# Second-half down product in fp16 terms with on-chip powers of two

## The chip, the cores and the metric

One core of one Trainium2 chip runs the whole program. The metric is the device time of one execution in microseconds (us). Three executions of the kernel before gave 1748.77, 1750.04 and 1750.48 us, median 1750.04. The result is float32 and is compared with the reference in float32, so the kernel carries each large product as two or three terms of fewer bits.

## The reference

2048 tokens of width 576 go through two branches, and a gate per token mixes them:

```python
g = sigmoid((x * gate_w).sum(-1, keepdims=True))
a = _A_ref(x, A_wq, A_wk, A_wv, A_wo, A_beta)      # attention in 4 segments, 32 heads of 18, with a memory
b = (silu(x @ w_gate) * (x @ w_up)) @ w_down       # 576 -> 4608 -> 576
return g * a + (1 - g) * b
```

The change is in the last product, `(silu * up) @ w_down`, for one half of the tokens.

## The kernel before

A first stage (up to about 233 us in the profiled execution) projects Q, K and V. Then the 4608 features are taken as 36 tiles of 128, and the tokens as two halves of 1024: the first half runs f = 0 to 35, then the second half does so. What follows calls them first and second half. A last stage multiplies the attention output by `wo`, mixes and stores.

For each feature tile f the loop does seven products (a Strassen scheme over gate and up, each 7 matmuls of 512 columns, in three fp16-term products plus a rest). Between them stand eight calls of `tick()`. A tick first issues what was put off to it (`defer(k, fn)` puts a function k ticks ahead), then some groups of the down product, then a step of the attention. So all engines' instructions stand in one program order which the ticks set; an engine works its own instructions strictly in that order. f mod 3 is called q below.

The row of the seven products and what reads them, with the lines of the profile: ScalarE copies the first sum (L1381), the second (L1384), the fourth (L1391) and the fifth (L1395); VectorE adds at L1388 and L1396; after the fifth product come the two Silu activations (L1398 and L1400). Silu and Exp stand in different activation tables, so in the second half each f then loads the Exp table back (`exp_table()`, L1297) for the attention. After the seventh product VectorE multiplies (L1406, L1407).

The down product of three feature tiles (a chunk, `CH = 3`) is done as 16 groups in the ticks of the next f with q = 0: 8 token tiles by two column parts of 320 and 256. Each group is 9 matmuls (3 tiles by 3 terms) into one of two banks, and VectorE adds the bank to the sum `ya` (L1098). The operands are pairs of fp32r terms: `hh`, `hl` from the product (ScalarE rounds at L1188 or L124, VectorE subtracts at L1189 or L125), and the two terms of `w_down`, made in the first half (L1070, L1071), stored to DRAM as `dc`, and fetched back in the second half by `d_fetch`. SyncE issues these transfers.

The attention runs in steps that a credit per tick paces: 0.76 of a step per tick without down groups, 1 with them. A step writes score tiles (L957 transposed scores, L846 scores) into banks 5, 6 and 7 in rotation (`ts_tile`); a bank is free again once ScalarE has taken the exponential (L961) or VectorE the maximum (L864, L854). GpSimd does the differences of the terms (L1058, L903).

`power(out, t)` (L140 to L146) turns a sum of squares into a power of two: one matmul with ones adds over the partitions, and four VectorE instructions on 128x1 make the power. The kernel before uses it for x and for the gate and up weights; `iw` holds the inverse scales.

## Time and profile before

| | us |
|---|---|
| median of 3 runs | 1750.04 |
| profiled execution, its own time | 1750.37 |
| its span, first to last instruction | 1748.7 |
| second half, from its first product to the end of f = 34 | 933 to 1646 |
| attention steps end, about | 1580 |

In the views, "idle before" is the time in which an engine stood still before an instruction, and the name after the arrow is what it waited for. Matmuls are pipelined: what one costs is the distance from one start to the next, not its printed duration. Weight loads (PEld) run beside matmuls. The profiler's clock row shows the TensorE clock as granted: 0.998 of full speed over the span.

### The profile page before, as it was taken

How to read it: one execution, taken by the hardware profiler on the slowest of the kernel's cores; microseconds unless marked ns; L12 is line 12 of the kernel's file. 1: busy time of each engine (PE TensorE's matmuls, PEld its weight loads, DVE VectorE, ACT ScalarE, POOL GpSimd, SP SyncE). 2: the span in 40 equal slices, each digit the busy share in tenths (PEclk: the TensorE clock that was granted, in tenths of full speed). 3: DMA queues.
4: the chain of work that ended last, by engine and by line, in shares of the span. 5: the costliest groups of instructions: out<-in, count | busy, mean ns of one | idle time of the engine just before them, and what ended most of it. 6: DMA issues, size and time to landing. Idle time of an engine off the chain costs nothing.

```text
span 1748.7 us, 34878 instructions
## 1 busy us (share of the span) xinstructions
PE 1714.6 (98%) x12241; PEld 1217.6 (70%) x12241; DVE 1326.4 (76%) x3239; ACT 1024.4 (59%) x1800; POOL 841.7 (48%) x1065
## 2 busy tenths in 40 slices
PE   9999999999999999999999999999999999999999
PEld 7889856666766676567656757766756766776699
DVE  6677676788878888888886877778778777775455
ACT  6756575767676666655754565566456466455411
POOL 3325552255545554665542764555546565553121
PEclk9999999999999999999999999999999999999999
DMA  8656776776687666545554477587577569654544
GB/s 284 224 211 225 237 244 206 224 234 191 179 247 225 205 186 193 185 142 153 169 165 150 123 181 182 132 207 170 125 185 196 143 147 210 167 125 129 184 137 139
DMA packets 341667, 321.89 MB, mean 184 GB/s; under 512 B 193396, under 2 KB 258676, under 8 KB 341492
## 3 DMA queue, kind: packets, MB, share of 16 engines
q1 hardware_dynamic: 341492, 319.67, 63.1%
q8 instruction: 96, 1.57, 0.4%
q14 instruction: 79, 0.65, 0.1%
HBM read 188.51 MB, written 104.86 MB: 168 GB/s over the span
## 4 chain that ended last, share of the span: by engine, by line
PE 79%; DVE 7%; ACT 5%; DMA 3%; issue 3%; SPq 2%; POOL 1%; DVEq 0%; ACTq 0%; POOLq 0%
PE bank L1304 33%; PE bank L1089 23%; PE bank L172 7%; PE bank L1307 5%; PE bank L846 4%; PE bank L957 2%; PE bank L985 2%; PE bank L987 1%; DMA stw<-q 1%; PE bank L919 1%; ACT L1297 1%; DVE xo L1242 1%; PE bank L460 1%; ACT L1398 1%; DMA wo__21835<-wc 0%
## 5 line engine op out<-in xcount | busy, mean ns | idle before, releaser
L1089 PE MATMUL bank<-dw,hh 128*128 128x320 f32 (+1 forms) x2304 | 510.0, 314 | 9.2 <-DVE ya L1098 7.0
L1089 PEld LDWEIGHTS bank<-dw,hh 128*128 128x128 f32 x2304 | 380.3, 190 | 35.0 <-DVE ya L1098 11.1
L1089 PE MATMUL bank<-dw,hl 128*128 128x320 f32 (+1 forms) x1152 | 341.0, 296 | 0.6 <-DVE hl L125 0.5
L1058 POOL TENSOR_TENSOR p<-pe,p 128x512 f16<-128x512 f32 x220 | 273.5, 1243 | 88.1 <-DVE p L1056 60.6
L961 ACT ACTIVATE pe<-bank 128x512 f32<-128x512 f32 x220 | 130.8, 594 | 222.3 <-PE bank L957 197.6
L1098 DVE TENSOR_TENSOR ya<-bank,ya 128x320 f32<-128x320 f32 x352 | 157.5, 453 | 90.1 <-PE bank L1089 87.2
L1089 PEld LDWEIGHTS bank<-dw,hl 128*128 128x128 f32 x1152 | 218.4, 190 | 1.1 <-DVE hl L125 1.1
L1307 PE MATMUL bank<-xr,rh 128*128 128x512 f16 x504 | 191.0, 379 | 0.0
L969 POOL TENSOR_SCALAR_AFFINE_SELECT pe<-pe 128x256 f32<-128x256 f32 (+1 forms) x220 | 92.4, 420 | 188.5 <-ACT pe L961 184.6
L864 DVE CUSTOM_DVE_ANT_0 junk<-bank,cm 128x128 bf16<-128x128 f32 (+2 forms) x352 | 169.8, 483 | 15.0 <-PE bank L846 10.0
L318 POOL TENSOR_TENSOR ws<-raw 128x256 f32<-128x256 f32 x72 | 67.5, 938 | 153.2 <-DMA raw<-in_wf_dram 91.3
L846 PE MATMUL bank<-kst,qst 108*128 108x512 bf16 (+3 forms) x512 | 125.2, 300 | 5.4 <-ACT pe L961 2.1
L1189 DVE TENSOR_TENSOR hl<-row,hh 128x512 fp32r<-128x512 f32 x120 | 110.9, 924 | 16.3 <-ACT hh L1188 16.1
L1056 DVE CAST p<-pe 128x512 f16<-128x512 f32 x220 | 108.2, 492 | 0.1
L1391 ACT ACTIVATE row<-bank 128x512 f32<-128x512 f32 x72 | 43.1, 598 | 106.8 <-PE bank L1307 106.6
L957 PE MATMUL bank<-qst,kst 111*128 111x512 bf16 (+3 forms) x352 | 104.2, 303 | 0.0
L1396 DVE TENSOR_TENSOR row<-bank,row 128x512 f32<-128x512 f32 x72 | 49.7, 691 | 70.7 <-ACT bank L1395 70.3
L172 PE MATMUL bank<-xo,qhi 128*128 128x512 f32 x288 | 91.9, 399 | 0.6 <-DVE xo L125 0.5
L1307 PEld LDWEIGHTS <-rh 128*128 128x128 f16 x504 | 49.3, 98 | 59.5
L1395 ACT ACTIVATE bank<-bank 128x512 f32<-128x512 f32 x72 | 41.9, 582 | 83.1 <-PE bank L1307 81.2
L416 POOL TENSOR_TENSOR q<-qr,q 128x512 bf16<-128x512 f32 x36 | 47.1, 1308 | 82.7 <-ACT q L415 70.2
L903 POOL TENSOR_TENSOR xo<-xr,xo 128x512 f16<-128x512 f32 x60 | 71.0, 1184 | 21.7 <-DVE xo L902 12.4
(1067 smaller groups left out, 4121.8 us busy)
## 6 DMA issues: line engine op xcount, KB each, us to landing
xo<-in_wf_dram SPq DMA_DIRECT2D x65, 320.0 KB
dc<-dw SPq DMA_DIRECT2D x36, 576.0 KB
dw<-dc SPq DMA_DIRECT2D x36, 576.0 KB
raw<-in_wf_dram SPq DMA_DIRECT2D x72, 256.0 KB
rh<-rc SPq DMA_DIRECT2D x72, 168.0 KB
draw<-in_wd_dram SPq DMA_DIRECT2D x36, 288.0 KB
xo<-in_xT_dram SPq DMA_DIRECT2D x33, 256.0 KB
vd<-vps SPq DMA_DIRECT2D x8, 912.0 KB
```

Source lines behind the costliest of these rows:

```text
L172: nc.tensor.matmul(t, st[n], mv[n], start=(n == 0), stop=(n == 13))
L846: nc.tensor.matmul(t[:, c:c + w], qs[:KR, pr, P * i:P * i + P], ks[:KR, pr, 0:w], start=True, stop=True)
L864: nc.vector.tensor_tensor_reduce(junk.bitcast(BF)[:, :w], t[:, c:c + w], cm[:, L - w:L], 1.0, -3.0e38, OP.add, OP.max, m[:, k:k + 1])
L957: nc.tensor.matmul(t[:, c:c + w], ks[:KR + 3, pr, P * j:P * j + P], qs[:KR + 3, pr, P * j:L], start=True, stop=True)
L961: nc.scalar.activation(pe, t, AF.Exp, scale=SCALE)
L1056: nc.vector.tensor_copy(p1, pe)
L1058: nc.gpsimd.tensor_sub(p2, pe, p1)
L1089: nc.tensor.matmul(t, p, q[:, cs], start=(f == CH * c and n == 0), stop=(f == CH * c + CH - 1 and n == 2))
L1098: nc.vector.tensor_add(ya[:, i, cs], t, ya[:, i, cs])
L1189: defer(k + 1, lambda: nc.vector.tensor_sub(lo, src, f32(hi)))
L1304: nc.tensor.matmul(t, w[:, p, z], x[z][:, q], start=first and n == 0, stop=False, skip_group_check=True)
L1307: nc.tensor.matmul(t, rem[:, RPOS[j]], XR[j], start=False, stop=True, skip_group_check=True)
```

## The change

In the second half the down product takes fp16 terms instead of fp32r ones. For this:

- `w_down` is no longer stored as terms in the first half. The second half loads the raw tiles, squares and sums them (`look`, ScalarE), finds a power of two for each chunk with `power`, and makes the fp16 terms `high` (ScalarE) and `low` (VectorE) in the free half of the same tile.
- The product `silu * up` is left in fp32 by the multiplies; each tile is squared and summed (`h_look`), and at q = 2 a second power of two per chunk is found and the terms of its tiles are made, 1024 columns at a time (`h_plan`).
- The eviction multiplies by the inverse of both powers, as one instruction with the add.
- The chunks of the second half are shifted: [0, 1], [2, 3, 4], ... [32, 33, 34], [35], so there are 13 instead of 12, and the last two are done in the last stage.

The first half keeps its fp32r product.

```diff
-    dc = dram.tile([FT, P, 2 * D], F32, name="dc")
...
-            defer(3, lambda: nc.sync.dma_start(dc[f], f32(d).rearrange("p a n -> p (a n)")))
...
+            if half:
+                inv = norms[fs[0]][2]
+                if fs[0] == 0:
+                    nc.vector.tensor_scalar_mul(ya[:, i, cs], t, inv)
+                else:
+                    nc.vector.scalar_tensor_tensor(ya[:, i, cs], t, inv, ya[:, i, cs], op0=OP.mult, op1=OP.add)
+                return
...
+        def d_plan(fs):
...
+            def load(f):
+                nc.sync.dma_start(at[f][0], wd[f])
+            def look(f):
+                nc.scalar.activation(dd[CH].bitcast(F16)[:, :D], at[f][0], AF.Square, accum_out=column(f % CH))
+            def high(f):
+                nc.scalar.activation(at[f][1][:, 0], at[f][0], AF.Copy, scale=sd)
+            def low(f):
+                nc.vector.scalar_tensor_tensor(at[f][1][:, 1], at[f][0], sd, at[f][1][:, 0], op0=OP.mult, op1=OP.subtract)
+            a, b = min(f % CH for f in fs), max(f % CH for f in fs) + 1
+            return load, look, lambda: total(sd, a, b), lambda: power(sd, ts_tile([P, 1])), high, low
+        def h_look(f, b, src):
+            nc.scalar.activation(junk, src, AF.Square, scale=iw[f // 4], accum_out=column(3 + 2 * (f % CH) + b))
+        def h_plan(fs):
...
+            def scales():
+                power(sh, ts_tile([P, 1]))
+                for i in at:
+                    nc.vector.tensor_mul(by[i], sh, iw[i])
+            def inverse():
+                nc.vector.tensor_mul(inv, sh, sd)
+                nc.vector.reciprocal(inv, inv)
+            def high(f):
+                t = terms(fp.tile([P, 2, L], F32R, name="hh" if f == FT - 1 else "hl"))
+                raw = hs[1, f]
...
+                nc.scalar.activation(hs[1, f][0], raw, AF.Copy, scale=by[f // 4])
+            def low(f):
+                hi, lo, raw = hs[1, f]
+                hs[1, f] = hi, lo
+                nc.vector.scalar_tensor_tensor(lo, raw, by[f // 4], hi, op0=OP.mult, op1=OP.subtract)
...
+        CHUNKS = [[f for f in range(c, c + CH) if 0 <= f < FT] for c in range(-1, FT, CH)]
...
+            if half and q == 0:
+                fs = CHUNKS[f // CH]
+                load, look, dt, dp, high, low = d_plan(fs)
+                plan += [((0, 1, 4)[n], lambda g=g, fn=load: fn(g)) for n, g in enumerate(fs)]
+                plan += [(5 + n, lambda g=g, fn=look: fn(g)) for n, g in enumerate(fs)]
+                plan += [(9, dt), (10, dp)]
+                for n, g in enumerate(fs):
+                    plan += [(11 + n, lambda g=g, fn=high: fn(g)), (12 + n, lambda g=g, fn=low: fn(g))]
...
+            if half and q == 2:
+                fs = CHUNKS[f // CH]
+                ht, hp, hi, high, low = h_plan(fs)
+                plan += [(2, ht), (3, hp), (4, hi)]
+                for n, g in enumerate(fs):
+                    plan += [(4 + n, lambda g=g, fn=high: fn(g)), (5 + n, lambda g=g, fn=low: fn(g))]
...
-                elif (q, k) in ((1, 0), (1, 2), (2, 1)):
-                    g = f - 1 if k == 0 else f
-                    ds[half, g] = d_fetch(g)
...
-            nc.vector.tensor_mul(sg0, xx, sg0)
-            nc.vector.tensor_mul(sg1, p5, sg1)
-            if q == CH - 1:
+            nc.vector.tensor_mul(hh[:, 0] if half else sg0, xx, sg0)
+            nc.vector.tensor_mul(hh[:, 1] if half else sg1, p5, sg1)
+            if half:
+                for b in range(2):
+                    defer(2 + b, lambda b=b, f=f, t=hh: h_look(f, b, t[:, b]))
+            elif q == CH - 1:
...
-            split_by(3, hh[:, 1], hl[:, 1], sg1)
+            if half == 0:
+                split_by(3, hh[:, 1], hl[:, 1], sg1)
```

Three places of the order. First, ScalarE at the boundary from f = 26 (q = 2) to f = 27 (q = 0) of the second half, before: `bank` is a product's sum, `pe` the attention's exponential, `row` a Silu, `bg` the dummy that goes with the Exp table.

```order
L1395 ACTIVATE bank_19691<-bank_19520 128x512
L961 ACTIVATE pe<-bank_19700 128x512
L1398 ACT_TABLE_LOAD
L1398 ACTIVATE row<-row,sc 128x512
L1400 ACTIVATE row<-bank_19611,sc 128x512
L1297 ACT_TABLE_LOAD
L1297 ACTIVATE bg<-idt 128x1
L961 ACTIVATE pe<-bank_19732 128x512
L1381 ACTIVATE bank_19758<-bank_19756 128x512
L124 ACTIVATE hh<-row 128x512
L961 ACTIVATE pe<-bank_19775 128x512
```

The same place of the change (L1486 was L1395, L960 was L961, L1489 and L1491 the Silus, L1368 was L1297, L1472 was L1381):

```order
L1486 ACTIVATE bank_19805<-bank_19629 128x512
L1172 ACTIVATE hl<-hh,sc 128x1024
L960 ACTIVATE pe<-bank_19818 128x512
L1489 ACT_TABLE_LOAD
L1489 ACTIVATE row<-row,sc 128x512
L1491 ACTIVATE row<-bank_19717,sc 128x512
L1368 ACT_TABLE_LOAD
L1368 ACTIVATE bg<-idt 128x1
L1172 ACTIVATE hl<-hh,sc 128x1024 x2
L960 ACTIVATE pe<-bank_19857 128x512
L1472 ACTIVATE bank_19882<-bank_19880 128x512
L1151 ACTIVATE junk,sc<-hh,sc 128x512
```

One `high` of the product's terms (L1172) now stands ahead of the Silu, and two stand behind the second table load, ahead of the exponential that came first there.

Second, VectorE at the same boundary in the change (L1177 is `low`, L1497 and L1498 were L1406 and L1407, L863 was L864). Before, the maxima L864 came straight after L1407.

```order
L1177 SCALAR_TENSOR_TENSOR hl<-hh,sc,hl 128x1024 x2
L1497 TENSOR_TENSOR hh<-bank_19805,row 128x512
L1498 TENSOR_TENSOR hh<-row 128x512
L1177 SCALAR_TENSOR_TENSOR hl<-hh,sc,hl 128x1024
L863 ISA junk,mb_2435<-bank_19859,cm 128x256
```

Two `low` now stand ahead of the closing multiplies and one behind them, ahead of the maxima.

Third, ScalarE at the boundary from f = 10 (q = 1) to f = 11 (q = 2) in the change; L1142 is `high` of `w_down`, L1151 is `h_look`, and the row that stood before between L1381 and the exponential was L1188 (`hh<-row`).

```order
L1486 ACTIVATE bank_14987<-bank_14810 128x512
L1142 ACTIVATE dw<-dw,sc 128x576
L960 ACTIVATE pe<-bank_14998 128x512
L1489 ACT_TABLE_LOAD
L1489 ACTIVATE row<-row,sc 128x512
L1491 ACTIVATE row<-bank_14852,sc 128x512
L1368 ACT_TABLE_LOAD
L1368 ACTIVATE bg<-idt 128x1
L1142 ACTIVATE dw<-dw,sc 128x576
L1472 ACTIVATE bank_15035<-bank_15033 128x512
L1151 ACTIVATE junk,sc<-hh,sc 128x512
L960 ACTIVATE pe<-bank_15051 128x512
```

Of the chunk's three `high` the first stands a few rows ahead of this piece, the second behind L1486 and the third behind the second table load. The `low` of the third stands on VectorE ahead of L1497.

More of the change, by code (lines that the diff above doesn't have):

```diff
@@ L1071, in d_split @@
             defer(2, lambda: nc.vector.scalar_tensor_tensor(d[:, 1], r, k, f32(d[:, 0]), op0=OP.mult, op1=OP.subtract))
-            defer(3, lambda: nc.sync.dma_start(dc[f], f32(d).rearrange("p a n -> p (a n)")))
-            return d
-        def d_fetch(f):
-            d = d_tile()
-            nc.sync.dma_start(f32(d).rearrange("p a n -> p (a n)"), dc[f])
             return d
         def down_part(t, g, a, b):
-            c, i, hf, hs, ws, half = g
+            fs, i, hf, half = g
             bl, k = divmod(i, 4)
             cs = (slice(0, 320), slice(320, D))[hf]
-            for f in range(CH * c + a, CH * c + b):
+            for f in fs[a:b]:
                 hh, hl = (z[:, bl, P * k:P * k + P] for z in hs[half, f])
-                d = ws[half, f]
+                d = ds[half, f]
                 dh, dl = d[:, 0], d[:, 1]
                 for n, (p, q) in enumerate(((hh, dh), (hh, dl), (hl, dh))):
-                    nc.tensor.matmul(t, p, q[:, cs], start=(f == CH * c and n == 0), stop=(f == CH * c + CH - 1 and n == 2))
+                    nc.tensor.matmul(t, p, q[:, cs], start=(f == fs[0] and n == 0), stop=(f == fs[-1] and n == 2))
         def down_end(t, g):
-            c, i, hf, hs, ws, half = g
+            fs, i, hf, half = g
             ya = yas[half]
             cs = (slice(0, 320), slice(320, D))[hf]
-            if c == 0:
+            if half:
[5 more added lines that the diff above has]
+                return
+            if fs[0] == 0:
                 nc.vector.tensor_copy(ya[:, i, cs], t)
@@ L1098, in down_end @@
                 nc.vector.tensor_add(ya[:, i, cs], t, ya[:, i, cs])
-            if c == FT // CH - 1 and hf and half == 0:
+            if fs[-1] == FT - 1 and hf:
                 stores.append((ffd[i], ya[:, i]))
@@ L1105, in down_groups, with column, terms @@
             for t, g in todo:
-                down_part(t, g, 0, CH - 1 if n > 1 else CH)
+                down_part(t, g, 0, len(g[0]) - (n > 1))
             for t, g in todo:
                 if n > 1:
-                    down_part(t, g, CH - 1, CH)
+                    down_part(t, g, len(g[0]) - 1, len(g[0]))
                 down_end(t, g)
+        norms = {}
+        dd = []
+        def column(k):
+            return sc[:, k:k + 1]
+        def terms(t):
+            return f32(t).rearrange("p a n -> p (a n)").bitcast(F16)
@@ new lines, in d_place @@
+        def d_place(f):
+            if f == FT - 1:
+                return fp.tile([P, D], F32, name="draw", bufs=2), dd[CH].bitcast(F16).rearrange("p (z n) -> p z n", z=2)
+            t = f32(dd[f % CH])
+            return t[:, 0], t[:, 1].bitcast(F16).rearrange("p (z n) -> p z n", z=2)
+        def d_plan(fs):
+            k = CHUNKS.index(fs) % 2
+            norms[fs[0]] = [column(20 + 8 * k + j) for j in range(5)]
+            sd = norms[fs[0]][0]
+            at = {f: d_place(f) for f in fs}
+            for f in fs:
+                ds[1, f] = at[f][1]
+            def load(f):
[8 more added lines that the diff above has]
+            return load, look, lambda: total(sd, a, b), lambda: power(sd, ts_tile([P, 1])), high, low
@@ new lines, in h_look @@
+        def h_look(f, b, src):
+            nc.scalar.activation(junk, src, AF.Square, scale=iw[f // 4], accum_out=column(3 + 2 * (f % CH) + b))
+        def h_plan(fs):
+            sd, sh, inv, *ks = norms[fs[0]]
+            at = sorted({f // 4 for f in fs})
+            by = {i: ks[n] for n, i in enumerate(at)}
+            a, b = 3 + 2 * min(f % CH for f in fs), 5 + 2 * max(f % CH for f in fs)
+            def scales():
[8 more added lines that the diff above has]
+                raw = hs[1, f]
+                hs[1, f] = [t[:, 2 * L * z:2 * L * z + 2 * L].rearrange("p (a n) -> p a n", a=2) for z in range(2)] + [raw]
+                nc.scalar.activation(hs[1, f][0], raw, AF.Copy, scale=by[f // 4])
[3 more added lines that the diff above has]
+                nc.vector.scalar_tensor_tensor(lo, raw, by[f // 4], hi, op0=OP.mult, op1=OP.subtract)
+            return lambda: total(sh, a, b), scales, inverse, high, low
@@ L1210, in beat, with feed @@
                         c_open()
-        def feed(half, f):
-            return [(f // CH, i, hf, hs, ds, half) for i in range(8) for hf in range(2)]
+        CHUNKS = [[f for f in range(c, c + CH) if 0 <= f < FT] for c in range(-1, FT, CH)]
+        def feed(half, fs):
+            return [(fs, i, hf, half) for i in range(8) for hf in range(2)]
         def x_second(new, z):
@@ L1317, in gated_mix @@
             if q == 0 and f:
-                groups += feed(half, f - 1)
+                groups += feed(half, CHUNKS[f // CH - 1] if half else list(range(f - CH, f)))
             plan = []
+            if half and f == 0:
+                dd += [d_tile() for _ in range(CH)] + [fp.tile([P, D], F32, name="draw", bufs=2)]
+            if half and q == 0:
[6 more added lines that the diff above has]
+                    plan += [(11 + n, lambda g=g, fn=high: fn(g)), (12 + n, lambda g=g, fn=low: fn(g))]
+            if half and f == FT - 2:
+                load, look, dt, dp, high, low = d_plan(CHUNKS[-1])
+                plan += [(o, lambda fn=fn: fn(FT - 1)) for o, fn in ((1, load), (5, look), (9, high), (10, low))]
+                plan += [(7, dt), (8, dp)]
+            if half and q == 2:
[4 more added lines that the diff above has]
+                    plan += [(4 + n, lambda g=g, fn=high: fn(g)), (5 + n, lambda g=g, fn=low: fn(g))]
             if nxt:
@@ L1375, in gated_mix @@
             hh = fp.tile([P, 2, L], F32R, name="hh")
-            hl = fp.tile([P, 2, L], F32R, name="hl")
-            hs[half, f] = hh, hl
+            if half:
+                hs[half, f] = hh = f32(hh)
+            else:
+                hl = fp.tile([P, 2, L], F32R, name="hl")
+                hs[half, f] = hh, hl
             a, y, xx = a_tile(), y_tile(), x_tile()
@@ L1405, in gated_mix @@
             seven(xx, 6, False)
-            nc.vector.tensor_mul(sg0, xx, sg0)
-            nc.vector.tensor_mul(sg1, p5, sg1)
-            if q == CH - 1:
+            nc.vector.tensor_mul(hh[:, 0] if half else sg0, xx, sg0)
+            nc.vector.tensor_mul(hh[:, 1] if half else sg1, p5, sg1)
+            if half:
+                for b in range(2):
+                    defer(2 + b, lambda b=b, f=f, t=hh: h_look(f, b, t[:, b]))
+            elif q == CH - 1:
                 defer(2, lambda t=(hh[:, 0], hl[:, 0], sg0): split(*t))
@@ L1417, in gated_mix @@
             if f == FT - 1:
-                groups += feed(half, f)
                 if half == 0:
+                    groups += feed(half, list(range(FT - CH, FT)))
                     for n in range(BREAK):
@@ L1425, in gated_mix @@
                     assert not groups
+        groups += feed(1, CHUNKS[-2]) + feed(1, CHUNKS[-1])
         while due:
@@ L1437, in gated_mix @@
         ops = None
+        total_, scales, inverse, high, low = h_plan(CHUNKS[-1])
+        last = {1: (total_, scales, inverse), 2: (lambda: high(FT - 1), lambda: low(FT - 1))}
         def downs(k):
@@ L1454, in gated_mix @@
                 nxt = c_tr(*tiles.pop(n))
+                for fn in last.get(n, ()):
+                    fn()
                 downs(2 if n else 4)
```

## The prediction

> **What bounds the kernel now.** I read the page first: how busy each engine is, and on which engine the chain that ended last lies.

> ```profile
> PE 1714.6 (98%) x12241; PEld 1217.6 (70%) x12241; DVE 1326.4 (76%) x3239; ACT 1024.4 (59%) x1800; POOL 841.7 (48%) x1065
> PE 79%; DVE 7%; ACT 5%; DMA 3%; issue 3%; SPq 2%; POOL 1%; DVEq 0%; ACTq 0%; POOLq 0%
> ```

> TensorE (PE) is busy all the time. Since a busy PE may still be waiting inside modelled ends, I read next what PE waited for in the second half alone (933 to 1646 us), the view of waits:

> ```profile
> PE bank L846 <- DMA kst<-stw: 2.0, 1, 2.0
> PE bank L1089 <- DVE ya L1098: 1.0, 3, 0.4
> PE bank L1304 <- DMA wo__21823<-wc: 0.7, 1, 0.7
> PE bank L846 <- ACT pe L961: 0.7, 2, 0.4
> ```

> These are the largest of seven, and all make some 5 us out of 713. So each microsecond taken from PE's own stream counts in full, and so does each new wait. Third, the windows of one chunk, f = 24, 25 and 26 (columns: PE, PEld, DVE, ACT, POOL busy, clock, DMA share):

> ```profile
> 1417.80:1454.10 36.30, 36.30 (x307) 28.91 (x305) 27.51 (x89) 16.30 (x28) 18.39 (x27) 1.00 0.55 117
> 1454.10:1465.70 11.60, 11.60 (x59) 5.51 (x58) 8.30 (x22) 8.62 (x15) 8.27 (x12) 1.00 1.04 295
> 1465.70:1480.20 14.50, 14.50 (x144) 7.98 (x143) 11.14 (x30) 10.45 (x18) 7.43 (x10) 1.00 0.88 187
> ```

> VectorE (DVE) works 46.95 of 62.4 us, ScalarE (ACT) 35.37. They are not full, but the slack lies in the long f with q = 0; at q = 1 and 2 they stand at 72 to 77%.

> **The matmuls.** The distances from start to start give the price of a column. These are PE's rows in a dense stretch:

> ```profile
> 1308.08 0.40 PE L1089 MATMUL bank<-dw,hh 128*128 128x256 f32 x2
> ...
> 1308.79 0.46 PE L1089 MATMUL bank<-dw,hh 128*128 128x320 f32 x2
> ...
> 1309.23 0.46 PE L1089 MATMUL bank<-dw,hh 128*128 128x320 f32 x2
> ...
> 1310.57 1.46 PE L1304 MATMUL bank<-xo,wo__16968 128*128 128x512 f16 x6
> 1311.86 0.38 PE L1307 MATMUL bank<-xr,rh 128*128 128x512 f16 x1
> ...
> 1479.99 0.22 PE L957 MATMUL bank<-qst,kst 111*128 111x128 bf16 x1
> 1480.05 0.27 PE L846 MATMUL bank<-kst,qst 108*128 108x256 bf16 x1
> ```

> Six fp32r matmuls of 256 columns take 0.71 us, 0.118 each; three of 320 take 0.44, 0.147 each; six fp16 ones of 512 take 1.29, 0.215 each, with a weight load for each. No fp16 row has 320 or 256 columns. If all of the 0.215 goes with the columns, they cost 0.134 and 0.1075; if I draw a line through the 512 columns and the 0.06 of the 128-column bf16 matmul, 0.138 and 0.112. The first saves 0.0118 a matmul on the mean, the second 0.0075; the second half's product has 36 x 8 x 2 x 3 = 1728 matmuls, so 13.0 to 20.4 us. I take 17.0, about the middle. The count of matmuls stays.

> [...]

> Added on PE: `power` twice for each of 13 chunks. One such call in the first half:

> ```profile
> 658.11 0.28 PE L141 MATMUL bank<-sc 128*128 128x1 f32 x2
> 658.25 0.38 PE L1304 MATMUL bank<-xo,wo__8278 128*128 128x512 f16 x1
> ```

> It holds PE for 0.14 us; 26 make 3.6. If PE reached one before its sum were ready it would wait, but the sum is put one tick ahead of it and the squares two (a tick at q = 1 or 2 is 1.5 to 1.8 us: 11.60 and 14.50 over eight), so I add nothing. PE alone: 1750.37 - 17.0 + 3.6 = 1737.0.

> The transfers (36 stores and 36 fetches of 576 KB gone, 36 loads of 288 KB new) cost nothing either way: no PE wait in the view is on `dw`, and the loads stand four to five ticks ahead of their use, the third three ticks in the long f. The 16 more evictions fall in the last stage, where VectorE has slack; uncovered they would be 16 times about half a microsecond, 8 us.

> **The work on ACT and DVE.** The nearest rows:

> ```profile
> L1188 ACT ACTIVATE hh<-row 128x512 fp32r<-128x512 f32 x120 | 74.3, 619 | 0.9 <-DVE row L1407 0.9
> L1189 DVE TENSOR_TENSOR hl<-row,hh 128x512 fp32r<-128x512 f32 x120 | 110.9, 924 | 16.3 <-ACT hh L1188 16.1
> ...
> L132 ACT ACTIVATE xr<-xr x8: 615/616/618, 58.1 to 120.2; 128x512 f32<-128x512 f32 x8
> L132 ACT ACTIVATION_READ_ACCUMULATOR xr<-xr x8: 185/186/188, 58.6 to 120.8; 128x1 f32 x8
> ...
> L1070 ACT ACTIVATE dw<-draw,sc x36: 761/762/768, 252.2 to 909.1; 128x576 fp32r<-128x576 f32 x36
> L1071 DVE SCALAR_TENSOR_TENSOR dw<-draw,sc,dw x36: 811/820/1889, 253.4 to 909.9; 128x576 fp32r<-128x576 f32 x36
> ...
> L1242 DVE SCALAR_TENSOR_TENSOR xo<-xo,sc,xo x10: 737/778/1785, 704.9 to 878.1; 128x512 f16<-128x512 f32 x10
> ```

> Per chunk ACT loses six roundings (6 x 0.62 = 3.7) and gets six squares with their sums (6 x 0.80 = 4.8), three squares of `w_down` (about 0.85 each, 2.6), its three `high` (0.76 each, 2.3) and three `high` of the product. These last have 1024 columns: 0.76 for 576, and twice a 512-column pass would be 1.24, so 1.15 each, 3.5. Net +9.5: ACT goes to 45 of 62 us. DVE loses six subtractions (5.5) and gets three `low` of `w_down` (0.82 each at the least), three of 1024 columns (1.27 from the 512-column and 576-column rows, up to 3.6 at twice the worst), and small ones and dearer evictions of some 3 us: about +4 to +5, to 52 of 62. Neither engine becomes full. If that were all, the time would be 1737.

> **Where it stands in the order.** An engine works in order, so I walk the boundary from f = 26 to 27. ACT, then PE, then DVE in the trace:

> ```profile
> 1476.51 0.58 ACT L1395 ACTIVATE bank<-bank 128x512 f32<-128x512 f32 x1 [1.20 <-PE bank L1307]
> ...
> 1477.62 1.28 ACT L1398 ACT_TABLE_LOAD   x1
> ...
> 1480.22 1.28 ACT L1297 ACT_TABLE_LOAD   x1
> 1481.52 0.20 ACT L1297 ACTIVATE bg<-idt 128x1 f32<-128x1 f32 x1
> 1481.63 0.58 ACT L961 ACTIVATE pe<-bank 128x512 f32<-128x512 f32 x1
> ```

> ```profile
> 1481.67 0.22 PE L957 MATMUL bank<-qst,kst 111*128 111x128 bf16 x1
> 1482.26 0.38 PE L846 MATMUL bank<-kst,qst 108*128 108x512 bf16 x1 [0.36 <-ACT pe L961]
> ```

> ```profile
> 1480.59 0.68 DVE L1407 TENSOR_TENSOR row<-row 128x512 f32<-128x512 f32 x1
> 1481.19 0.42 DVE L864 CUSTOM_DVE_ANT_0 junk<-bank,cm 128x256 bf16<-128x256 f32 x1
> ```

> From L1395 on, ACT runs without a gap to the exponential at 1481.63, and PE already waits for it: the score matmul at 1482.26 needs that bank. The change puts one `high` of 1.15 us behind L1395 and two more behind the Exp table load, all ahead of this exponential. It ends 3 x 1.15 = 3.4 us later, and PE waits 3.3 us more (0.1 for overlaps). Each `high` is needed only by the down groups ticks later, but everything behind it pays: exponentials, copies, squares. On DVE the second `low` waits for the second `high` (done at 1480.22 + 1.15 + 1.28 + 0.2 + 1.15 = 1484.0), and the two multiplies, the last `low` and the maxima stand behind it: 1.27 + 0.6 + 0.6 + 1.3 after 1484.0 is 1487.8 against 1481.19. So a boundary whose first step has no exponential waits for a maximum instead, with only three score banks; I price it alike. Before attention ends (about 1580) there are ten such boundaries, f = 2, 5, ... 29: 33 us.

> From q = 1 to q = 2 the same goes for `w_down`. At f = 10 to 11:

> ```profile
> 1147.35 0.58 ACT L1395 ACTIVATE bank<-bank 128x512 f32<-128x512 f32 x1 [1.14 <-PE bank L1307]
> ...
> 1151.06 1.28 ACT L1297 ACT_TABLE_LOAD   x1
> ...
> 1153.50 0.57 ACT L961 ACTIVATE pe<-bank 128x512 f32<-128x512 f32 x1
> ...
> 1154.12 0.38 PE L846 MATMUL bank<-kst,qst 108*128 108x512 bf16 x1
> ```

> The first `high` fits the 1.14 us gap. The second moves the table load by 0.66 to 0.76, the third follows it (to about 1153.9), its `low` takes 0.82, the first multiply 0.6, the square that reads its result 0.8, and only then comes the exponential: it ends at about 1156.7 instead of 1154.07, on which the matmul at 1154.12 follows at once. That is 2.6 us. It needs a transposed score in the first step, which I count for half of ten boundaries: 13 us. In the others the maxima are late by some 3 us, about what three banks cover.

> Sum: 1737.0 + 33 + 13 - 2 (present waits of the same kind, which the new ones swallow) = **1781 us**. The profiled execution is 0.33 above the median, which I leave.

> **The rivals.**
> - *PE's stream alone decides.* The three score banks and the ticks' distance cover the late exponentials; all new work falls in slack. For it: the second half waits for only 5 us in 713 although the Exp table load stands in the same chain, and DVE and ACT stay under 84%. Against it: the recorded wait of 0.36 us, which says that at such a boundary the cover is used up. It decides if the `high` cost no PE wait above 1.3 us a chunk (13.4 / 10). With the two ends of the saving, 1750.37 + 3.6 - 20.4 and - 13.0, that is 1734 to 1741, faster.
> - *Half of it is absorbed.* Each wait of PE gives ACT and DVE time to catch up, so later boundaries find more slack: 10 x 1.3 instead of 46 - 2. Time about 1750, between 1745 and 1762.
> - *The `low` are stretched by GpSimd.* L1242 has 0.737 us at the least and 1.785 at the worst; two `low` in the chain of ten boundaries by 1.05 us more are 21 us. Time about 1802. [...] Against the full price: the median is 0.778.
> - *fp16 is not quicker here*, as the columns might cost 0.118 and 0.147 in any type. The 0.215 row speaks against it; 1798 with the waits.

> **How the numbers follow.** The chain of the `high` 0.60; PE alone 0.23; half absorbed 0.10 (0.02 faster, 0.05 the same, 0.03 slower); GpSimd 0.05; no gain in fp16 0.02. A measurement of this kernel tells about 0.2% from no change, 1746.5 to 1753.5. Faster 0.25, same 0.05, slower 0.70. The likeliest's own range is 1765 to 1795 (a wait of 2 to 4.5 us at each boundary); with PE alone below and most of the GpSimd case above, 1735 to 1803.

> **What would show it.** Right: distances of about 0.136 and 0.110 us in the new down matmuls; in the view of waits for the second half, score matmuls behind exponentials and maxima with 30 to 50 us in all, most of them right after q = 2; the `high` of 1024 columns behind the Exp table load. Wrong: PE waits under 15 us in the second half (then the first rival), or waits at `power` or at the loads, which I priced at nothing.

## The result and the profile after

The changed kernel takes **1836.47 us** (median of 4 runs, 1834.60 to 1838.64) against 1749.40 for the kernel before (4 runs, 1747.52 to 1750.48): a ratio of 1.0499, 95% interval 1.0481 to 1.0518. It is 5% slower. The prediction had the sign, but its time, 1781, is 55 us short, and the measured time lies outside its range.

The profiled execution spans 1832.9 us, 84.2 more than the 1748.7 before. The page's engine line and the shares of its chain:

```profile
PE 1729.2 (94%) x12293; PEld 1165.5 (64%) x12293; DVE 1386.7 (76%) x3429; ACT 1122.7 (61%) x2016; POOL 845.2 (46%) x1065
PE 70%; ACT 12%; DVE 11%; issue 4%; DMA 2%; POOL 1%; SPq 0%; DVEq 0%; ACTq 0%; POOLq 0%
```

PE was busy for 98% of the span and is now at 94%; ACT and DVE have gone from 5% and 7% of the chain to 12% and 11%. Neither is full on the mean. That points to the order of the work, and the loss has to be looked for where the change is. These are the windows of the second half (from its first feature tile to the start of f = 35), first of the kernel before, then of the changed one, each followed by the stretch from f = 35 to the end (columns as in the prediction's windows):

```profile
933.00:1646.00 713.00, 707.42 (x5678) 474.32 (x5677) 526.95 (x1470) 400.83 (x666) 377.78 (x496) 1.00 0.64 160
1646.00:1748.70 102.70, 98.66 (x721) 92.18 (x721) 58.26 (x111) 20.51 (x48) 20.66 (x26) 1.00 0.48 159
```

```profile
931.20:1712.90 781.70, 714.98 (x5675) 423.29 (x5674) 570.47 (x1619) 491.03 (x867) 379.73 (x498) 0.97 0.55 134
1712.90:1832.90 120.00, 107.55 (x776) 92.59 (x774) 74.41 (x152) 28.93 (x62) 18.65 (x24) 0.97 0.39 126
```

Two things are to be seen. PE's idle time (length less busy) in the second half went from 5.6 to 66.7 us, and in the last stretch from 4.0 to 12.5. And the clock column fell from 1.00 to 0.97: PE was busy for 7.6 us *more* in the second half, though its matmuls had become cheaper. The prediction's sum has no term for the clock.

What PE waited for in the second half (us in total, times, longest):

```profile
PE bank L1375 <- ACT bank L1472: 17.8, 8, 3.5
PE bank L845 <- ACT pe L960: 17.5, 11, 3.5
PE bank L956 <- DVE acc L929: 10.9, 3, 4.0
PE bank L845 <- DVE mb L853: 5.8, 2, 4.3
PE bank L845 <- DVE mb L863: 3.2, 3, 2.9
```

First evictions (L1472) and exponentials (L960) on ACT, reductions and maxima on DVE: four releasers. Whether they have one cause is for the experiments; the boundary that the prediction walked through, f = 26 to 27, shows how one such wait comes about. ACT, then PE, then DVE, in time:

```profile
1534.99 1.28 ACT L1368 ACT_TABLE_LOAD   x1
1536.29 0.20 ACT L1368 ACTIVATE bg<-idt 128x1 f32<-128x1 f32 x1
1536.40 2.17 ACT L1172 ACTIVATE hl<-hh,sc 128x1024 f16<-128x1024 f32 x2
1538.47 0.57 ACT L960 ACTIVATE pe<-bank 128x512 f32<-128x512 f32 x1
```

```profile
1534.13 1.24 PE L1375 MATMUL bank<-xo,wo__19720 128*128 128x512 f16 x5
...
1535.42 0.22 PE L956 MATMUL bank<-qst,kst 111*128 111x128 bf16 x1
1539.10 0.58 PE L845 MATMUL bank<-kst,qst 108*128 108x512 bf16 x1 [3.46 <-ACT pe L960]
1539.48 0.52 PE L956 MATMUL bank<-qst,kst 111*128 111x384 bf16 x1
1539.80 2.76 PE L1375 MATMUL bank<-xo,wo__19738 128*128 128x512 f16 x6
```

```profile
1537.56 1.28 DVE L1177 SCALAR_TENSOR_TENSOR hl<-hh,sc,hl 128x1024 f16<-128x1024 f32 x1 [3.45 <-ACT hl L1172]
1538.76 0.68 DVE L1497 TENSOR_TENSOR hh<-bank,row 128x512 f32<-128x512 f32 x1
```

The two `high` (L1172) run behind the table load and ahead of the exponential; the score matmul waits 3.46 us for it; and the `low` (L1177) has waited as long, with the closing multiply behind it. That is the prediction's chain. What it did not say stands in the last PE row: six matmuls of 512 columns take 2.76 us, where five took 1.24 just before. In steps, that is from 0.215 to 0.427 us each. The windows around the wait show why (the clock is the third number from the end):

```profile
1535.00:1537.90 2.90, 0.64 (x4) 0.28 (x3) 0.34 (x1) 2.89 (x4) 0.00 (x0) 0.99 0.70 209
1537.90:1544.70 6.80, 5.35 (x14) 1.97 (x14) 6.59 (x17) 4.21 (x9) 1.52 (x2) 0.50 0.02 2
1544.70:1548.00 3.30, 3.30 (x24) 2.13 (x23) 2.67 (x9) 1.87 (x3) 2.99 (x7) 1.00 0.90 214
```

From 1537.9 to 1544.7 us PE was granted half its clock. The record of the clock has twelve such stretches in the second half, of 3.41 or 6.83 us, 51.2 us in all (PE is busy in 45.7 of them), and two in the last stretch (6.8 us); the kernel before has none in either.

### The profile page after: what moved, and what is told of

The parts are those of the page before. It is cut to its first block, busy times and chain, and to the rows that moved or that the text cites. A ratio compares the mean times of both kernels' runs of the same rounds, so it can differ in the third digit from the quotient of the medians.

```text
span 1832.9 us, 35290 instructions
## 1 busy us (share of the span) xinstructions
PE 1729.2 (94%) x12293; PEld 1165.5 (64%) x12293; DVE 1386.7 (76%) x3429; ACT 1122.7 (61%) x2016; POOL 845.2 (46%) x1065
## 4 chain that ended last, share of the span: by engine, by line
PE 70%; ACT 12%; DVE 11%; issue 4%; DMA 2%; POOL 1%; SPq 0%; DVEq 0%; ACTq 0%; POOLq 0%
PE bank L1375 28%; PE bank L1082 20%; PE bank L171 7%; PE bank L1378 5%; PE bank L845 3%; ACT L1368 2%; PE bank L956 2%; ACT L1489 2%; PE bank L984 1%; ACT hl L1172 1%; DVE junk L863 1%; ACT row L1489 1%; ACT row L1491 1%; ACT pe L960 1%; DVE hh L1497 1%
## 5 line engine op out<-in xcount | busy, mean ns | idle before, releaser
L1082 PE MATMUL bank<-dw,hl 128*128 128x256 f16 (+2 forms) x2256 | 403.3, 290 | 7.1 <-DVE ya L1093 2.4
L1082 PE MATMUL bank<-dw,hh 128*128 128x320 f32 (+1 forms) x1152 | 255.0, 314 | 7.4 <-DVE ya L1098 6.4
L960 ACT ACTIVATE pe<-bank 128x512 f32<-128x512 f32 x220 | 130.1, 592 | 203.5 <-PE bank L956 185.6
L1082 PEld LDWEIGHTS <-hl 128*128 128x128 f16 x1680 | 164.7, 99 | 65.7 <-issue 6.9
L1082 PEld LDWEIGHTS bank<-dw,hh 128*128 128x128 f32 x1152 | 189.4, 189 | 21.7 <-DVE ya L1098 8.6
L968 POOL TENSOR_SCALAR_AFFINE_SELECT pe<-pe 128x256 f32<-128x256 f32 (+1 forms) x220 | 96.4, 438 | 215.0 <-ACT pe L960 192.1
L863 DVE CUSTOM_DVE_ANT_0 junk<-bank,cm 128x128 bf16<-128x128 f32 (+2 forms) x352 | 169.8, 482 | 28.1 <-ACT junk L1151 17.0
L1093 DVE SCALAR_TENSOR_TENSOR ya<-bank,sc,ya 128x320 f32<-128x320 f32 x192 | 96.9, 513 | 60.6 <-PE bank L1082 59.9
L1082 PEld LDWEIGHTS bank<-dw,hl 128*128 128x128 f32 x576 | 108.9, 189 | 1.8 <-DVE hl L124 1.8
L1098 DVE TENSOR_TENSOR ya<-bank,ya 128x320 f32<-128x320 f32 (+1 forms) x176 | 78.1, 451 | 25.2 <-PE bank L1082 23.6
L1486 ACT ACTIVATE bank<-bank 128x512 f32<-128x512 f32 x72 | 41.9, 582 | 78.6 <-PE bank L1378 77.2
L857 POOL TENSOR_SCALAR nb<-mb 128x2 f32<-128x2 f32 (+1 forms) x100 | 36.5, 365 | 107.4 <-DVE mb L853 103.0
```

The source lines that it names most:

```text
L863: nc.vector.tensor_tensor_reduce(junk.bitcast(BF)[:, :w], t[:, c:c + w], cm[:, L - w:L], 1.0, -3.0e38, OP.add, OP.max, m[:, k:k + 1])
L960: nc.scalar.activation(pe, t, AF.Exp, scale=SCALE)
L968: nc.gpsimd.affine_select(d, d, pattern=pat, compare_op=OP.is_ge, fill=0.0, base=0, channel_multiplier=-1)
L1082: nc.tensor.matmul(t, p, q[:, cs], start=(f == fs[0] and n == 0), stop=(f == fs[-1] and n == 2))
L1093: nc.vector.scalar_tensor_tensor(ya[:, i, cs], t, inv, ya[:, i, cs], op0=OP.mult, op1=OP.add)
```

## The experiments

Theory T: each low and high term stands in a queue that runs in order, ahead of work that PE needs soon; this makes PE wait, at some twenty places by 1.5 to 4.3 us, and a wait of about 3 us also costs the clock of the next 3.41 or 6.83 us. Its rivals: the amount of added work on ACT and DVE (W); the finding of the powers (P, S); the scratch tile that the squares of h share with the attention's maxima (J); that the half clock costs nothing (N); that the fp16 product is itself the loss (F). All runs were timed beside the kernel before, which stayed between 1748.39 and 1749.55. The table has, for the second half, PE's idle time by the windows and the length of the half-clock stretches:

| kernel | median us | ratio to before, 95% | idle us | half clock us |
|---|---|---|---|---|
| before | 1749.40 | | 5.6 | 0 |
| changed | 1836.47 | 1.0481 to 1.0518 | 66.7 | 51.2 |
| e1 own tile for the squares | 1831.99 | 1.0457 to 1.0492 | 62.6 | 58.0 |
| e2 no finding of powers | 1820.14 | 1.0390 to 1.0421 | 61.8 | 44.4 |
| e3 h's highs on DVE | 1844.68 | 1.0532 to 1.0564 | 68.1 | 61.4 |
| e4 down weights' chain earlier | 1814.29 | 1.0357 to 1.0392 | 55.8 | 44.4 |
| e5 matmuls that fill the waits | 1824.12 | 1.0414 to 1.0464 | 26.1 | 6.8 |
| e6 h's terms spread | 1802.14 | 1.0283 to 1.0326 | 49.5 | 10.2 |
| e7 all moved | 1771.68 | 1.0111 to 1.0148 | 31.4 | 3.4 |
| e8 spread further | 1810.77 | 1.0336 to 1.0373 | 53.1 | 34.1 |
| e9 two at step 8 | 1776.56 | 1.0129 to 1.0170 | 35.3 | 6.8 |
| e10 two early | 1771.11 | 1.0098 to 1.0145 | 30.4 | 3.4 |
| e11 e10 without finding powers | 1748.38 | 0.9992 to 1.0011 | 15.7 | 0 |
| e12 no terms at all | 1726.88 | 0.9865 to 0.9898 | 5.5 | 0 |

### The squares' own tile (e1)

In the trace of the changed kernel DVE's maxima waited 17.0 us on the squares of h, which write the same scratch tile:

```profile
DVE junk L863 <- ACT junk L1151: 17.0, 15, 2.7
```

```diff
-nc.scalar.activation(junk, src, AF.Square, scale=iw[f // 4], accum_out=column(3 + 2 * (f % CH) + b))
+t = junk if f > 31 else dd[CH].bitcast(F16)[:, :L]
+nc.scalar.activation(t, src, AF.Square, scale=iw[f // 4], accum_out=column(3 + 2 * (f % CH) + b))
```

> The squares of h for its total go to a tile of their own up to f = 31, in place of the tile that the attention's maxima on VectorE write too. In the changed kernel's trace VectorE's maxima waited 17.0 us in 15 places on those squares, and TensorE waited about 10 us on maxima. Theory T (the place of the high and low terms in ACT's and DVE's queues makes waits of about 3 us on TensorE, and these halve its clock): the waits behind the table load stay, so 1820 to 1833 us. Rival J (the shared tile is what costs): 1795 us or less. Against 1836.47 us of the changed kernel.

1831.99, in T's range. That wait is gone from the list, and the time is 4.5 us less. J is out as the main cause; it was a real but small one, which the prediction had not seen.

### Without finding the powers (e2)

```diff
 def look(f):
-    nc.scalar.activation(dd[CH].bitcast(F16)[:, :D], at[f][0], AF.Square, accum_out=column(f % CH))
+    pass
...
-return load, look, lambda: total(sd, a, b), lambda: power(sd, ts_tile([P, 1])), high, low
+return load, look, lambda: None, lambda: None, high, low
...
-    nc.scalar.activation(junk, src, AF.Square, scale=iw[f // 4], accum_out=column(3 + 2 * (f % CH) + b))
+    pass
...
-    power(sh, ts_tile([P, 1]))
...
```

> Leaves out the finding of the powers: the squares, the totals, the power matmuls with their bit operations and the inverse; all scales are the constant 1, so the output is not the reference's. The high and low terms, their places and the closing multiply stay. Theory T (place of the high and low terms): the waits at the start of every third feature tile stay at 3 us and over, the shorter ones two tiles later shrink; 1795 to 1825 us. Rival P (finding the powers is what costs, by 51 squares on ACT of 0.7 to 0.9 us and the chain through power): 1765 us or less.

1820.14, in T's range; P is out. The largest waits of PE are those of the changed kernel:

```profile
PE bank L1372 <- ACT bank L1470: 17.8, 8, 3.5
PE bank L845 <- ACT pe L960: 15.6, 7, 3.5
```

T's own detail, that the shorter waits would shrink, did not come: the mean length of the third feature tile of a chunk only went from 16.0 to 15.7 us.

### The highs on VectorE (e3)

```diff
-nc.scalar.activation(hs[1, f][0], raw, AF.Copy, scale=by[f // 4])
+nc.vector.tensor_scalar_mul(hs[1, f][0], raw, by[f // 4])
```

> h's high terms are made on VectorE in place of ScalarE, at the same places of the program; nothing is left out. Nothing of them then stands behind the exponential's table load on ScalarE, and no low waits for another engine; VectorE gets 36 operations of 1024 elements more, 0.6 to 1.2 us each, 22 to 43 us in all. Theory T: the waits of about 3.6 us at ten boundaries shrink to 1 us or less and most of the half-clock windows go; 1775 to 1805 us. Rival W (the amount of work on VectorE is what holds TensorE): 1836 us or more.

1844.68: slower, as W had it and T had not. DVE's rows at the same boundary show what T, as stated then, had missed:

```profile
1533.81 0.73 DVE L1172 TENSOR_SCALAR hl<-hh,sc 128x1024 f16<-128x1024 f32 x1
...
1535.38 1.46 DVE L1177 SCALAR_TENSOR_TENSOR hl<-hh,sc,hl 128x1024 f16<-128x1024 f32 x1
1536.76 0.77 DVE L1172 TENSOR_SCALAR hl<-hh,sc 128x1024 f16<-128x1024 f32 x1
1537.57 1.28 DVE L1177 SCALAR_TENSOR_TENSOR hl<-hh,sc,hl 128x1024 f16<-128x1024 f32 x1
1538.77 0.90 DVE L1172 TENSOR_SCALAR hl<-hh,sc 128x1024 f16<-128x1024 f32 x1
1539.59 0.68 DVE L1497 TENSOR_TENSOR hh<-bank,row 128x512 f32<-128x512 f32 x1
```

The table load no longer delays a `high`, and a `high` takes 0.75 us instead of 1.13. But three of them and two `low` now stand ahead of the closing multiply (L1497), with a third `low` behind it, ahead of the maxima. So the wait only changes its releaser: the exponential is on time again (0.36 us, as in the kernel before), and PE waits for a maximum instead:

```profile
1538.07 0.38 PE L845 MATMUL bank<-kst,qst 108*128 108x512 bf16 x1 [0.36 <-ACT pe L960]
...
1542.92 0.37 PE L956 MATMUL bank<-qst,kst 111*128 111x256 bf16 x1 [2.80 <-DVE mb L863]
```

The table load is not the point; what stands ahead of the multiplies, maxima and exponentials is. From here on T means that. The run alone does not tell T from W, since it also adds work to DVE.

### Moving the same work: e4, e6, e7

These move the same instructions on the same engines, so W expects nothing of them. The numbers are ticks, counted from the start of the f in which the plan is made, eight to an f: 8 is the first tick of the next f. (The expectations call them steps.) e4 moves the chain of `w_down`:

```diff
-plan += [((0, 1, 4)[n], lambda g=g, fn=load: fn(g)) for n, g in enumerate(fs)]
-plan += [(5 + n, lambda g=g, fn=look: fn(g)) for n, g in enumerate(fs)]
-plan += [(9, dt), (10, dp)]
+plan += [((0, 0, 1)[n], lambda g=g, fn=load: fn(g)) for n, g in enumerate(fs)]
+plan += [(3 + n, lambda g=g, fn=look: fn(g)) for n, g in enumerate(fs)]
+plan += [(6, dt), (7, dp)]
...
-    plan += [(11 + n, lambda g=g, fn=high: fn(g)), (12 + n, lambda g=g, fn=low: fn(g))]
+    plan += [((9, 9, 10)[n], lambda g=g, fn=high: fn(g)), ((10, 11, 12)[n], lambda g=g, fn=low: fn(g))]
```

> The down weights' chain alone is moved two to three steps earlier (their loads, squares, total, power, high and low terms), so that no high of theirs stands behind the table load of the silu and exponential; the same instructions on the same engines. Theory T (place): the waits at the start of every third tile of three (about 2.2 us at ten boundaries) shrink by half or more with the half-clock windows behind them, those at the first tile stay; 1800 to 1822 us. Rival W (the amount of work on ACT and DVE): within 1830 to 1840, no change against 1836.47.

e6 spreads the terms of h, with no other change:

```diff
-    plan += [(4 + n, lambda g=g, fn=high: fn(g)), (5 + n, lambda g=g, fn=low: fn(g))]
+    plan += [((4, 7, 8)[n], lambda g=g, fn=high: fn(g)), ((5, 8, 9)[n], lambda g=g, fn=low: fn(g))]
```

> h's three high terms of a chunk are made at steps 4, 7 and 8 in place of 4, 5 and 6, their low terms at 5, 8 and 9 in place of 5, 6 and 7: only the first pair is still ahead of VectorE's closing multiplies, and no high stands between the exponential's table load and those. The same instructions on the same engines. Theory T: the waits of about 3.6 us at the ten boundaries shrink to 1.5 us or less and with them most of their half-clock windows; 1780 to 1812 us. Rival W (the amount of work on ACT and DVE): 1830 us or more; so also rival Q, by which the exponentials stay as late as before, since the highs then stand just behind them and ahead of the next tile's first eviction.

e7 has both, the tile of e1, and the last stage's steps apart:

```diff
-last = {1: (total_, scales, inverse), 2: (lambda: high(FT - 1), lambda: low(FT - 1))}
+last = {1: (total_,), 2: (scales, inverse), 3: (lambda: high(FT - 1), lambda: low(FT - 1))}
```

> All moves together: the down weights' chain earlier, h's high and low terms at 4, 7, 8 and 5, 8, 9, the squares of h in a tile of their own, and in the last stage the total, the power and the terms of the last feature tile at three successive steps. Nothing is left out. Theory T: both groups of waits, and the last stage's 7 us of waits on the power, mostly go, and the half-clock windows with them; 1745 to 1785 us. Rival W: 1820 us or more.

1814.29, 1802.14 and 1771.68: all in T's ranges, and all outside W's (and e6 outside that of Q, which its expectation names). The traces show that each move takes away the waits that it was aimed at, and no others. I count the waits that begin within 9.5 us of a feature tile's first matmul. At the ten boundaries to q = 0 (f = 3 to 30) PE waits 34.5 us in the changed kernel, 34.6 in e4 and 20.0 in e6; at the nine to q = 2 (f = 5 to 29) it waits 19.9, 1.0 and 19.9 us.

The gains nearly add up: 22.2 (e4), 34.3 (e6), 4.5 (e1) and, in e7's last stretch, 7.3 (120.0 to 112.7 us, to the end of the span) make 68.3, where e7 gained 64.8. In e7 that last stretch has this in place of the changed kernel's waits at `power` (6.7 us, 3 times):

```profile
PE bank L140 <- DVE sc L137: 1.6, 2, 0.8
```

The waits left in e6 are of the same two kinds as before, but none is over 3.0 us, and only 10.2 us of half clock are left:

```profile
PE bank L845 <- ACT pe L960: 17.2, 13, 3.0
PE bank L1375 <- ACT bank L1472: 14.6, 9, 2.5
```

### Filling the waits (e5)

What does the clock alone cost? Here nothing is moved and no wait is taken away; PE is given matmuls without use just ahead of where it waits:

```diff
+if half and f and k == 0 and q != 1:
+    t = pair_tile()
+    for _ in range((14, 0, 9)[q]):
+        nc.tensor.matmul(t, cm[:, 0:P], cm, start=True, stop=True)
 beat(k, half)
```

> Adds matmuls that compute nothing used: 14 of 512 columns in bf16 (0.215 us each, 3.0 us) at the start of the first feature tile of three, 9 (1.9 us) at the start of the third, just ahead of where TensorE waited; everything else as in the changed kernel. Theory C (the half clock after each wait costs some 27 us in the second half): the waits that remain are under 1 us, the matmuls fill time that was idle, the half-clock windows in the second half go, and the time falls by 15 to 30 us: 1805 to 1822 us. Rival N (the half-clock windows cost nothing, since TensorE isn't the bound just there): 1836 us or more, up to 1860 if the waits stay behind the added matmuls.

1824.12: 12.4 us *faster*, with 253 matmuls, some 54 us of useless work (an estimate, at 0.215 us each as in the rows of 512 columns above), added to the second half. It lies 2 us outside C's range, and on the other side of N's. The windows of the second half:

```profile
931.40:1706.60 775.20, 749.07 (x5906) 443.03 (x5927) 568.82 (x1619) 491.39 (x867) 379.57 (x498) 1.00 0.55 135
```

The clock is 1.00. The trace misses one added matmul of each group, 22 in all, so of the 26.1 us of idle time 4.7 are really busy, and busy time is 753.8. Of the added 54 us some 45 fell into what was idle (66.7 to 21.4), some 9 did not, and were paid. Without them PE was busy for about 699 us against 714.98: 16 us for the clock. That is near half of the 38.8 us for which PE worked in the half-clock stretches that went, 19. So N is out. The clock is a cost of its own, which adds to the wait that caused it.

### Too far, and two more places (e8, e9, e10)

Could the terms be placed better still? All three keep e7's other moves, move the squares of every third tile three ticks later, and place the terms of h anew. In e8:

```diff
-    plan += [((4, 7, 8)[n], lambda g=g, fn=high: fn(g)), ((5, 8, 9)[n], lambda g=g, fn=low: fn(g))]
+    a, b = (((3, 8, 9), (4, 9, 10)), ((3, 4, 5), (4, 5, 7)))[f == FT - 1]
+    plan += [(a[n], lambda g=g, fn=high: fn(g)), (b[n], lambda g=g, fn=low: fn(g))]
...
-    defer(2 + b, lambda b=b, f=f, t=hh: h_look(f, b, t[:, b]))
+    defer((5 if q == 2 and f < FT - 1 else 2) + b, lambda b=b, f=f, t=hh: h_look(f, b, t[:, b]))
```

> As e7 with h's terms moved once more: the first high at step 3, ahead of both table loads and where ScalarE's trace of e7 is idle, the other two at 8 and 9, behind the attention's exponential of step 7; the low terms at 4, 9 and 10; the squares of every third tile three steps later; the last chunk's terms at 3, 4, 5 and 4, 5, 7. Nothing is left out. Theory T: e7's remaining waits on the exponentials (14.8 us on TensorE) and on the next tile's first eviction (6.3 us) fall by half or more; 1748 to 1764 us. Rival W (what is left is the amount of work on VectorE and ScalarE, with VectorE at 0.8 of the time): within 5 us of e7's 1771.68.

1810.77, a plain miss of both ranges: 39 us slower than e7, where W had it within 5. Its largest waits in the second half:

```profile
PE bank L1082 <- DVE hl L1178: 32.0, 15, 3.8
PE bank L845 <- ACT pe L960: 8.0, 10, 1.7
```

The waits on the exponentials did fall, from 14.8 to 8.0. But the down products start at 10 (tick 2 of the next f), and the last `low` (L1178 here) is put at that very tick; PE now waits for it, at up to 3.8 us, and the half clock is back with 34.1 us. e9 has `(3, 8, 8), (4, 8, 9)` in place of e8's first two tuples, e10 `(3, 4, 8), (4, 5, 9)`.

> As e8, but the third high back at step 8 with the second, and the low terms at 4, 8 and 9 in place of 4, 9 and 10, one step before the down products that e8 made wait (34.6 us of waits on the low terms in e8's trace). Theory T: those waits go to 5 us or less, and the exponential of step 7 still stands directly behind the table load; 1748 to 1765 us. Rival W: 1765 us or more, by waits that only move on to the next tile's first eviction and exponentials, since two highs and two lows then stand in one step.

> As e8, but the highs at 3, 4 and 8 and the low terms at 4, 5 and 9: two pairs ahead of the silu, one at the next tile's start. Theory T: no wait on low terms in the down products; the exponential of step 7 comes 1.1 us later than in e9 and TensorE waits for it 1 to 1.5 us at some boundaries; 1755 to 1772 us. Rival W: the same as e9 within 3 us, since the work is the same.

1776.56 and 1771.11. e9 missed T's range by 12 us and lies in W's, which expected the waits only to move on; in its second half and last stage PE still waits for the low terms:

```profile
PE bank L1082 <- DVE hl L1178: 11.8, 9, 2.0
```

e10 is inside T's range, and 5.5 us below e9, where W had 3 at most. But the intervals of e7 and e10, and of e7 and e9, overlap: the three don't rank. Between too early and one tick too late there is a plateau at some 1772 to 1777, and no placing that I tried leaves it. Its lower end is 1.2% above the kernel before.

### What is left (e11, e12)

e11 is e10 with e2's edits. e12 is the changed kernel with those edits and without `high` and `low`, those of `w_down` too:

```diff
 def high(f):
-    t = terms(fp.tile([P, 2, L], F32R, name="hh" if f == FT - 1 else "hl"))
+    t = still[f % CH]
...
-    nc.scalar.activation(hs[1, f][0], raw, AF.Copy, scale=by[f // 4])
 def low(f):
-    nc.vector.scalar_tensor_tensor(lo, raw, by[f // 4], hi, op0=OP.mult, op1=OP.subtract)
+    pass
...
+    still += [terms(fp.tile([P, 2, L], F32R, name="hl")) for _ in range(CH)]
+    for t in still + [d_place(g)[1] for g in range(CH)] + [d_place(FT - 1)[1]]:
+        nc.gpsimd.memset(t, 0.5)
...
```

> e10's places of the terms (highs at 3, 4, 8, lows at 4, 5, 9, the down weights' chain earlier, the last stage's steps apart), with the finding of the powers left out as in e2: no squares, totals, power matmuls, scales or inverse; all scales are the constant 1, so the output is not the reference's. Theory T with the work behind it: what e10 still loses (43.6 us of excess on TensorE in the second half) is ScalarE and VectorE being full, so with 51 squares of 0.7 to 0.9 us less it falls below e2's gain of 16 us by no more than half: 1748 to 1763 us. Rival S (the squares fill only gaps once the terms are placed well): 1765 to 1773 us.

> Leaves out all that the change adds on ScalarE and VectorE for the second half but the closing multiply: no squares, powers, high or low terms; the down product takes constants in fp16, so the output is not the reference's. ScalarE and VectorE have less to do than in the kernel before too, whose splits of h are gone. Theory T (the matmuls save what was priced, and all the loss is from making the terms): 1725 to 1741 us, the half-clock windows of the second half gone. Rival F (fp16 products, their closing multiply or their loads cost by themselves): 1750 us or more.

1748.38 and 1726.88, both in T's ranges; S and F are out. The second half of e10, e11 and e12, one line from each kernel's windows:

```profile
930.20:1655.50 725.30, 694.87 (x5676) 417.46 (x5675) 577.87 (x1621) 490.25 (x869) 392.09 (x498) 1.00 0.59 144
```

```profile
930.50:1633.20 702.70, 687.03 (x5630) 411.99 (x5629) 560.98 (x1469) 419.18 (x663) 390.78 (x498) 1.00 0.62 149
```

```profile
930.40:1619.00 688.60, 683.13 (x5630) 412.37 (x5629) 485.88 (x1402) 365.11 (x596) 373.86 (x505) 1.00 0.63 152
```

ACT has 490, 419 and 365 us of work in these, DVE 578, 561 and 486, and PE idles for 30.4, 15.7 and 5.5. The finding of the powers (squares on ACT, totals, `power`, scales) costs 22.7 us once the terms are well placed, more than the 16.3 it cost in e2: less work on ACT and DVE does help, but it is the second cause, not the first.

So the change's 87 us come apart, by medians, from the top: 65.4 are the places (changed to e10), with the clock and the scratch tile of e1 in them; 22.7 are the finding of the powers (e10 to e11); 21.5 the making of the terms, against none (e11 to e12); and the fp16 product itself gains 22.5 (before to e12). The last two are somewhat too large, by as much as the splits of h cost, which e12 lacks and the kernel before has; no run shows that alone.

## Why the prediction was wrong, point by point

- **The saving in the matmuls: right.** Predicted 17.0 us, from distances of 0.136 and 0.110. These are PE's rows of one and of nine such matmuls in the changed kernel:

```profile
1545.88 0.30 PE L1082 MATMUL bank<-dw,hl 128*128 128x320 f16 x1
...
1549.82 1.39 PE L1082 MATMUL bank<-dw,hl 128*128 128x320 f16 x9
```

  Eight distances in 1.39 - 0.30 us are 0.136 each; for 256 columns the median over the trace is 0.109. Against the medians before, 0.147 and 0.120, that is 0.011 x 1728 = 19.0 us. That lies between the two readings, nearer to the upper one (20.4). e12 bears the sum out: for PE alone 1737 was forecast, and 1726.88 plus 3.6 for the 26 `power` that it leaves out is 1730.5; 2 of the 6.5 us between are the matmuls, and the splits of h that it lacks too may be the rest.
- **The first boundary, q = 2 to q = 0: right in mechanism, near in size.** 3.3 us at ten boundaries, 33 us; in the trace each of the ten has waits of 2.6 to 4.3 us, 34.5 in all, and the walk from f = 26 to 27 came about row by row. That the sum fits so well is in part luck: every boundary was priced like the one walked, while others of the ten wait for a first eviction, a maximum or a reduction, none of which was worked out. e3 corrects one part: not the table load but the place ahead of multiplies, maxima and exponentials decides. e6, which changes that alone, gains 34.3.
- **The second boundary, q = 1 to q = 2: right in mechanism, mis-sized.** 2.6 us were counted at half of ten boundaries, 13 us. The trace has 1.3 to 3.0 us at each of the nine from f = 5 on, 19.9 in all. Where no transposed score stands in the first step, PE waits for something else that is late. At f = 11, the boundary that was walked, the wait is 3.02 us:

```profile
1174.88 0.59 ACT L960 ACTIVATE pe<-bank 128x512 f32<-128x512 f32 x1
1175.52 0.38 PE L845 MATMUL bank<-kst,qst 108*128 108x512 bf16 x1 [3.02 <-DMA wo__15108<-wc]
```

  The view names a load of `wo`, which this matmul does not read. The exponential ended at 1175.47, 0.05 us before the matmul began, as in the walk. In e4 these nine waits are down to 1.0 us: it is this chain.
- **What was priced at nothing: wrong in two places.** After the end of the attention one more boundary (f = 32 to 33) waits 3.5 us, for the first eviction on ACT, which the prediction did not count. In the last stage PE idles for 12.5 us instead of 4.0, above all at `power`:

```profile
PE bank L140 <- DVE sc L137: 6.7, 3, 4.0
```

  "The sum is put one tick ahead" held inside the loop (1.5 us there, 3 times) but not behind it, where total and `power` stand directly behind each other. The waits at the loads were nothing, as forecast: the 3.0 us that the view puts down to `wo` are the exponential's at f = 11.
- **The step that failed: the sum has each wait at its own length only.** It takes 33 + 13 - 2 = 44 us of waits and stops there. Measured, PE's idle time in the second half rose by 61.1 (66.7 less 5.6), and the clock's share was left out whole. The balance of the second half gives it: PE's busy time rose by 7.6; 1536 cheaper matmuls are -16.9, 48 that the new chunks move to the last stage -6.4, 23 `power` +3.2, and that leaves 27.7. The record of the clock says 22.8, half of the 45.7 us for which PE worked at half clock. In the last stretch busy time rose by 8.9, of which the moved matmuls and the cheaper ones are 4.3 and three `power` 0.4; 4.2 are left, and the record says 3.3. So the clock took 26 us by its record, and 32 at most. The 6 us between may be a matter of counting, an estimate: the last matmul ahead of a wait counts with its printed 0.38 us, not with the 0.215 from start to start, and the second half has 33 more waits than before, which makes up to 5 us.

  Of the 54 us by which the profiled execution (1834.60) lies above 1781, the clock with this rest is 32, the size and number of the waits in the second half 17 and the last stage 8.5, less 2.0 for the matmuls and 1.8 for a shorter first half. The rest of the balance is in the 32, so this sum has to close; what stands by itself is the clock's record and the idle time.
- **The rivals.** PE's stream alone (0.23): out, its sign was wrong, the cover of three score banks does not hold. Half absorbed (0.10): out; the waits did not become rarer along the half. The `low` stretched by GpSimd (0.05): in the kernel before, of the 14 instructions of L1242 on VectorE six took 1.65 to 1.79 us, and all six began while a GpSimd instruction ran; eight took 0.74 to 0.81, two of them begun so. In the changed kernel, of the 36 `low` on the product's terms two took longer than 1.29 us (1.47 and 2.07), and both began while a GpSimd instruction ran, as did two of the other 34. Together these two make 1.0 us, where the rival had 21; out. fp16 not quicker: out. The time is above them all. The likeliest's mechanism was at work, and something that follows from it had no entry in the range.

## What to carry to other kernels

When PE has been busy throughout, look for the clock behind a new wait of about 3 us, and price the wait at its length plus what that costs: here eight of nine waits of 3.0 us or more had 3.41 or 6.83 us at a clock of 0.50 behind them, which is up to 1.7 or 3.4 us more; some twenty places, each harmless by itself, became 5%. Work that is needed only some ticks later still has a price at its place in the queue: name what stands behind it, and what is the last step at which it may stand, for one step further (e8) costs as much as the one too early. And a change that shifts work from the bounding engine to engines that are busy for 56% (ACT) and 74% (DVE) of the second half has to be compared with a version that leaves this work out (e12): the gain of 22.5 us was there, but making the terms cost more than that, even where they stood best.
